# A fused gated recurrence and soft mixture of experts on one core: where two sigmoids stand in ScalarE's order, and a last weight loaded in three parts

## The chip, the cores and the metric

The kernel runs on one core of a Trainium2 chip. The metric is the time of one execution on the device, in microseconds (us). TensorE (PE, with its weight loads as PEld), VectorE (DVE), ScalarE (ACT) and GpSimd (POOL) each work through an order of their own; SyncE (SP) issues most of the transfers.

## The reference

For each of 4 batches of 5056 tokens with 256 channels, the first part is a recurrence along the tokens; the second part sends all 20224 tokens through 32 slots of 8 small experts and back.

```python
sig = 1.0 / (1.0 + np.exp(-f_logit))
f = lower_bound + (1.0 - lower_bound) * sig
i = 1.0 - f
for t in range(S):
    h = f[:, t] * h + i[:, t] * x[:, t]
    y[:, t] = h
...
logits = x @ phi                                # x: the recurrence's output, (20224, 256)
d = softmax of logits over the tokens           # each slot's weights
slot_input = d.T @ x
slot_out[e] = maximum(slot_input[e] @ w1[e], 0) @ w2[e]      # 8 experts, 4 slots each
c = softmax of logits over the 32 slots
out = c @ slot_out
```

## The kernel before

**Units.** The recurrence is cut into 40 units. A unit is a stretch of 512 tokens of one batch (`G`; `n_grp` is 10, and `B` is 4). Two units that are neighbours in number form a pair: one tile of logits `f_t`, one of `x_t` and one of gates `s_t` hold both of them. From unit 8 to 31 the units are "long" (`long`, line 177): a pair is 1024 neighbouring tokens of one batch, and each of its two tiles comes in one transfer (line 201). The tiles `f_t` and `x_t` have three buffers each.

**One unit's way through the engines.**

- `load` (line 194), for a pair, on SP's queue: `f_t`, then `x_t`. SP issues them in order; the one waits until a buffer of `f_t` is free, and that of `x_t` until one of `x_t` is.
- `gate` (line 217), on ACT, for a pair: the sigmoid of the negative logits into `s_t` (2048 elements in each partition).
- `enter` (line 227), on POOL, for each unit: `u_t = s_t * x_t`.
- `s_to_channels` (line 259) and `u_to_channels` (line 265), on PE: transposes of `s_t` and `u_t` into PSUM (`sp`, one buffer for a pair; `up`, two). For a long unit `u_to_channels` reads the `u_t` of both units of its pair (`half_to_channels`, line 253).
- `decay` (line 276), on ACT, for a pair: two instructions that make the decay `a` out of `sp` (line 285).
- `scan` (line 296), on DVE: two scans of 512 steps, out of `a` and `up`, into `h`.
- `to_tokens` (line 310), on PE, and `keep_tokens` (line 326), on DVE or ACT: `h` transposed back (`hp`, one buffer) and copied to `ht`. ACT has it for odd units, but for units with n mod 8 equal to 1 or 4 the two change places.
- `logits` (PE), `exps` (ACT, once for each two groups, line 356), `weights_to_tokens` (PE transposes `ep`, DVE copy `et`, line 371), `slots` (PE, line 397): the slot sums.

`idle` (line 170) and `spin` (line 142) issue matmuls whose results nobody reads.

**The order.** The instructions are issued in the order of the Python loop over n (line 469), and each engine keeps that order. In round n of the part that matters here, ACT gets: on an even n the gate of pair n+4, if n is at least `2 * B` = 8; on an odd n the decay of n+1 and then, if n is below 8, the gate of n+3. Then follow `exps` (for group 1 in round 9), and at the end of the round `keep_tokens(n - 1)`. POOL gets `enter(n + 3)`, then the weight loads that `W_AT` (line 148) names for this round. PE gets `to_tokens(n - 1)`; on an even n `s_to_channels` of n+2 and n+3; `u_to_channels(n + 1)`; `idle`; logits; and after the scan the transposes of the weights and the slot sums. Exps and sigmoids use different function tables of ACT, so a table load stands ahead of each change between them.

**The weights.** `load_w` (line 128) issues the 16 expert weights from POOL, one float32 array to one bf16 tile each. The last two go into a buffer of `f_t` (`w_t`). The last one, number 15, is loaded in two halves, of four chunks each along the hidden dimension (line 137). Six weights, 10 to 15, are issued in round 36; behind them POOL fills `hid` and `wide` with zeros (lines 565, 566) and copies `left` (line 390). Each half of weight 15 is read at the end of the expert part, by the matmuls of line 663: 16 for weight 14, then 16 for weight 15, two for each chunk, chunk 0 first.

**After that** all output rows are made in a stage of its own and stored (lines 687 to 793).

Of the kernel before, what the change touches and what calls it, by code (L numbers as in the profile page):

```python
# [18 lines left out]
def kernel(  # L19
# [11 lines left out]
    B, S, D = x.shape  # L31
    E = moe_w1.shape[0]
# [5 lines left out]
    FC = F // P  # L38
# [45 lines left out]
    def rep_constants(b):  # L84
        blk = ident_f[ds(b * NS, NS), ds(b * NS, NS)]
        nc.gpsimd.tensor_copy(rep[ds(b * NS, NS)], blk.unsqueeze(1).broadcast_to([NS, B, NS]))
# [41 lines left out]
    def load_w(i):  # L128
        if i < E:
            nc.gpsimd.dma_start(out=w1_sb[i], in_=w1_r[i])  # L130
        else:
            if i == 2 * E - 2:
                t = ld.tile([P, 2, R, D], F32, name="w_t", tag="f_t")
                t = t.rearrange("p u r d -> p (u r d)").bitcast(BF16).rearrange(
                    "p (e f d) -> p e f d", e=2, f=FC)
                w2_sb.extend(t[:, i] for i in range(2))
            k = FC // 2 if i == 2 * E - 1 else FC
            for f in range(0, FC, k):
                nc.gpsimd.dma_start(out=w2_sb[i - E][:, ds(f, k)], in_=w2_r[i - E][:, ds(f, k)])


# [13 lines left out]
    with tc.tile_pool(name="sp2", bufs=3) as sp2, \  # L155
# [38 lines left out]
        def load(n, k=2):  # L194
            for src, dst, tag in ((f_logit, fs, "f_t"), (x, xs, "x_t")):
                if n % 2 == 0:
                    dst[n // 2] = ld.tile([P, 2, R, D], F32, name=tag, tag=tag)
                t = dst[n // 2]
                if long(n):
                    g, b = place(n)  # L200
                    nc.sync.dma_start(
                        out=t.rearrange("p u r d -> p (u r) d"),
                        in_=src[b, ds(first(g), 2 * G)].rearrange("(p r) d -> p r d", r=2 * R))
                elif n // B == odd:
                    b, t0 = n % B, first(odd)
                    nc.sync.dma_start(
                        out=t[:, 0, R3],
                        in_=src[ds(b, 2), ds(t0 + P * R3, L)].rearrange("b t d -> t b d"))
                    for m in range(2):
                        nc.sync.dma_start(  # L210
                            out=t[:, m, ds(0, R3)],
                            in_=src[b + m, ds(t0, P * R3)].rearrange("(p r) d -> p r d", r=R3))
                else:
                    for m in range(n, n + k):
                        nc.sync.dma_start(out=t[:, ds(m % 2, 1)], in_=tokens(src, m, 1))

        def gate(n, k=2):
            if n % 2 == 0:
                sts[n // 2] = sp2.tile([P, 2, R, D], BF16, name="s_t", tag="s_t")
            s_t, f_t = sts[n // 2][:, ds(n % 2, k)], fs[n // 2][:, ds(n % 2, k)]  # L220
            if n // B == odd:
                m = (R + R3) * D
                s_t = s_t.rearrange("p u r d -> p (u r d)")[:, :m]
                f_t = f_t.rearrange("p u r d -> p (u r d)")[:, :m]
            nc.scalar.activation(s_t, f_t, ACT.Sigmoid, scale=-1.0)  # L225
# [33 lines left out]
        def s_to_channels(n):  # L259
            if n % 2 == 0:  # L260
                pss[n // 2] = psp.tile([P, 2, P, R], F32, name="sp", tag="sp")
            to_channels(n, pss[n // 2][:, n % 2], sts[n // 2][:, n % 2],
                        sts[n // 2][:, 0, R3])
# [88 lines left out]
        def exps(g):  # L352
            gs = batch_of(g)
            if g == gs[-1]:
                T = sum(rows(i) for i in gs) * R
                nc.scalar.activation(etall[:, ds(first(gs[0]), T)], lgs[0][:, :T], ACT.Exp,
                                     accum_out=csum[:, ds(g, 1)])
# [45 lines left out]
        def unit(f, m):  # L403
            if 0 <= m < n_unit:
                f(m)

        def group(f, m):
            if 0 <= m < n_unit and m % B == B - 1:
                f(m // B)
# [39 lines left out]
                                     skip_group_check=True)  # L449

        AHEAD = 6
        for n in range(SINGLE):
            load(n, 1)
        lb_constants()
# [14 lines left out]
        for n in range(n_unit):  # L469
            if n < SINGLE - 2:  # L470
                if n:
                    unit(to_tokens, n - 1)
                    unit(u_to_channels, n + 1)
                s_to_channels(n + 2)
                if n + 3 < SINGLE:
                    gate(n + 3, 1)
                decay(n + 2, 1)
                if n + 3 == SINGLE:
                    gate(n + 3)
                if n % 2 == 0:  # L480
                    unit(load, n + AHEAD)
                unit(enter, n + 3)
                rep_constants(n)
            else:
                end = n >= n_unit - 6
                if n % 2 == 0:
                    unit(load, n + AHEAD)
                    if n == SINGLE - 2:
                        to_tokens(n - 1)
                        keep_tokens(n - 1)  # L490
                    if not end and n >= 2 * B:
                        unit(gate, n + 4)
                else:
                    unit(decay, n + 1)
                    if n < 2 * B:
                        gate(n + 3)
                    if n == n_unit - 5:
                        gate(n + 3)
                        exps(odd - 1)
                if not end and n != n_unit - 7:  # L500
                    group(exps, n - 2)

                unit(enter, n + 3)
                for _ in range(W_AT.get(n, 0)):
                    load_w(w_next[0])
                    w_next[0] += 1

                if n == n_unit - 2:
                    unit(u_to_channels, n + 1)
                if n != SINGLE - 2:  # L510
                    unit(to_tokens, n - 1)
                if n == n_unit - 2:
                    keep_tokens(n - 1)
                if n % 2 == 0:
                    unit(s_to_channels, n + 2)
                    unit(s_to_channels, n + 3)
                if n != n_unit - 2:
                    unit(u_to_channels, n + 1)
                if n in (n_unit - 5, n_unit - 4):
                    idle(8)  # L520
                elif n == SINGLE - 2:
                    idle(4, True)
                elif n < n_unit - 4 and n % (2 * B) in (1, 5, 6, 7):
                    idle({6: 8, 7: 9}.get(n, 5 if n % 2 else 3))
                if n == n_unit - 2:
                    tail = psp.tile([P, 2, G], F32, name="tail", tag="sp")
                    rs_ps = tail[:, 0, ds(0, n_grp * R * B)].rearrange(
                        "p (q b) -> p q b", b=B)
                    late_ps, odd_ps = (
                        tail[:, 1].bitcast(BF16)[:, ds(i * R * P, R * P)].rearrange(  # L530
                            "p (r s) -> p r s", r=R) for i in range(2))
                    logits(odd)
                    exps(odd)
                    slots(odd - 1)
                    spin(tail[:, 1], 1, G)
                    odd_weights()
                elif not end and long(n - 1):
                    if n % B == 0:
                        g = (n - 1) // (2 * B) * 2
                        for i in range(2):  # L540
                            logits(g + i, [2, 3] if n % (2 * B) == 0 else [0, 1])
                elif not end:
                    group(logits, n - 1)
            if n == n_unit - 1:
                logits(last, [0, 1, 2])
                late_exps([0, 1, 2])
                row_sums(0)
                late_weights([0, 1, 2], nc.scalar.copy)

            unit(scan, n)  # L550
            if n not in (SINGLE - 2, n_unit - 2):
                unit(keep_tokens, n - 1)
            if n == n_unit - 3:
                weights_to_tokens(odd - 1)
                slots(odd - 2)
            elif not n >= n_unit - 6:
                group(weights_to_tokens, n - 3)
                batch(slots, n - 4, 0)
                batch(slots, n - 4, 1)
                if n > 2 * B and n % (2 * B) == 3:  # L560
                    idle(6)
# [126 lines left out]
    with tc.tile_pool(name="pout", bufs=4, space=PSUM) as pout, \  # L688
# [95 lines left out]
        end = len(blocks) - 1  # L784
# [39 lines left out]
```

## Time and profile before

| | |
|---|---|
| median of 4 runs | 200.77 us (200.63 to 202.54) |
| the profiled execution | 200.63 us, of which 198.9 us are the span from its first to its last instruction |
| mean granted TensorE clock | 0.855 |
| PE busy | 152.2 us (77%) |
| DVE busy | 143.3 us (72%) |
| ACT busy | 138.8 us (70%) |
| POOL busy | 102.6 us (52%) |
| DMA | 70.77 MB, 356 GB/s on the mean |
| the two scans' line 303, DVE, with and without a start value | 86.8 us and 9.4 us, some 1.2 us for each of 80 |

Read the times of a timeline as: start in us from the beginning of the span, how long, engine, line, operation, written tile and read tiles, shape, how many instructions lie in this row; in square brackets how long the engine was idle before, and what ended that. Rows of PE overlap a little, since matmuls are pipelined. In a row of windows each engine's busy time in that stretch stands with its number of instructions, then the granted TensorE clock, the DMA share and the GB/s.

### The profile page before, as it was taken

How to read it: one execution, taken by the hardware profiler on the slowest of the kernel's cores; microseconds unless marked ns; L12 is line 12 of the kernel's file. 1: busy time of each engine (PE TensorE's matmuls, PEld its weight loads, DVE VectorE, ACT ScalarE, POOL GpSimd, SP SyncE). 2: the span in 40 equal slices, each digit the busy share in tenths (PEclk: the TensorE clock that was granted, in tenths of full speed). 3: DMA queues.
4: the chain of work that ended last, by engine and by line, in shares of the span. 5: the costliest groups of instructions: out<-in, count | busy, mean ns of one | idle time of the engine just before them, and what ended most of it. 6: DMA issues, size and time to landing. Idle time of an engine off the chain costs nothing.

```text
span 198.9 us, 3495 instructions
## 1 busy us (share of the span) xinstructions
PE 152.2 (77%) x1330; PEld 108.8 (55%) x1330; DVE 143.3 (72%) x164; ACT 138.8 (70%) x195; POOL 102.6 (52%) x77
## 2 busy tenths in 40 slices
PE   0587496988998989899897987989989999960000
PEld 0365375766785767667685866667953633310000
DVE  1669888489989999999989999634158877850000
ACT  3688679499999998999997595623067889990000
POOL 2489577984987788874969969650030000000000
PEclk9999969699999999999999999999985555555555
DMA  6999999999999999999999999999429999999995
GB/s 181 413 419 422 428 428 424 424 427 343 397 432 419 415 328 420 430 408 323 398 419 391 226 213 213 214 215 210 84 95 419 424 440 422 422 448 438 428 422 214
DMA packets 14304, 70.77 MB, mean 356 GB/s; under 512 B 1728, under 2 KB 2752, under 8 KB 10320
## 3 DMA queue, kind: packets, MB, share of 16 engines
q1 hardware_dynamic: 11664, 62.13, 75.7%
q0 software_dynamic: 2480, 8.42, 21.2%
q8 instruction: 10, 0.16, 0.3%
q14 instruction: 6, 0.05, 0.1%
q10 hardware_dynamic: 144, 0.00, 0.0%
HBM read 58.23 MB, written 20.71 MB: 397 GB/s over the span
## 4 chain that ended last, share of the span: by engine, by line
PE 45%; DVE 25%; DMA 8%; issue 4%; ACT 4%; POOL 2%; SPq 0%; ACTq 0%; DVEq 0%; POOLq 0%
DVE h L303 18%; PE op L751 12%; DMA f_t<-in_f_logit_dram 8%; PE hp L316 5%; DVE ht L333 5%; PE sp L251 5%; PE up L257 4%; PE lg L347 3%; PE slot_ps L173 2%; PE op L702 2%; POOL u_t L236 2%; PE so_ps L663 2%; PE tail L144 2%; PE slot_ps L397 2%; ACT oc L762 1%
## 5 line engine op out<-in xcount | busy, mean ns | idle before, releaser
L236 POOL TENSOR_TENSOR u_t<-s_t,x_t 128x1024 bf16<-128x1024 bf16 (+1 forms) x39 | 82.5, 2127 | 24.3 <-ACT s_t L225 9.6
L303 DVE TENSOR_TENSOR_SCAN h<-a,h,up 128x512 bf16<-128x512 f32 (+1 forms) x72 | 86.8, 1251 | 6.0 <-PE up L257 4.8
L225 ACT ACTIVATE s_t<-f_t 128x2048 bf16<-128x2048 f32 (+2 forms) x23 | 38.4, 1669 | 7.9 <-DMA f_t<-in_f_logit_dram 7.4
L316 PE MATMUL hp<-ident_f,h 128*128 128x128 f32 (+1 forms) x160 | 29.8, 311 | 9.1 <-DVE ht L333 7.8
L316 PEld LDWEIGHTS hp<-ident_f,h 128*128 128x128 f32 (+1 forms) x160 | 23.0, 208 | 17.6 <-DVE ht L333 12.5
L251 PE MATMUL sp<-ident_f,s_t 128*128 128x128 f32 x144 | 21.2, 290 | 10.5 <-ACT s_t L225 7.9
L285 ACT ACTIVATE a<-sp,nomlb 128x1024 f32<-128x1024 bf16 x24 | 25.4, 1113 | 0.8 <-PE sp L251 0.6
L751 PE MATMUL op<-slot_bd,etall 64*128 64x512 bf16 x62 | 25.0, 621 | 0.3 <-ACT oc L762 0.2
L762 ACT ACTIVATE oc<-op,rrow 128x256 f32<-128x256 f32 x60 | 22.7, 486 | 2.1 <-PE op L751 1.6
L251 PEld LDWEIGHTS sp<-ident_f,s_t 128*128 128x128 f32 x144 | 17.4, 150 | 12.2 <-issue 5.9
L756 DVE TENSOR_TENSOR oc<-op,rrow 128x1024 f32<-128x1024 f32 x16 | 19.3, 1222 | 5.3 <-PE op L751 5.3
L292 ACT ACTIVATE a<-sp,nomlb 128x512 f32<-128x512 bf16 (+2 forms) x22 | 17.8, 857 | 3.9 <-PE sp L251 3.5
L257 PE MATMUL up<-ident_f,u_t 64*128 64x64 f32 x192 | 17.2, 229 | 2.2 <-POOL u_t L236 2.2
L751 PEld LDWEIGHTS <-etall 64*128 64x128 bf16 x62 | 9.0, 155 | 14.8 <-issue 12.7
L173 PE MATMUL slot_ps<-rep,ident 128*128 128x256 bf16 x115 | 17.1, 285 | 0.0
L257 PEld LDWEIGHTS up<-ident_f,u_t 64*128 64x128 f32 x192 | 13.7, 138 | 5.9 <-POOL u_t L236 2.5
L333 ACT COPY ht<-hp 128x512 f32<-128x512 f32 (+1 forms) x18 | 10.5, 581 | 7.5 <-PE hp L316 7.4
L333 DVE COPY ht<-hp 128x512 f32<-128x512 f32 (+1 forms) x22 | 14.7, 667 | 0.8 <-PE hp L316 0.8
L173 PEld LDWEIGHTS <-ident 128*128 128x128 bf16 x119 | 10.9, 103 | 2.8 <-issue 0.6
L303 DVE TENSOR_TENSOR_SCAN h<-a,up 128x512 bf16<-128x512 f32 x8 | 9.4, 1210 | 2.6 <-ACT a L292 1.9
L347 PE MATMUL lg<-h,phi 128*32 128x512 bf16 (+1 forms) x80 | 10.1, 412 | 0.0
L251 PE MATMUL up<-ident_f,u_t 128*128 128x128 f32 x48 | 9.3, 324 | 0.8 <-POOL u_t L236 0.8
(105 smaller groups left out, 147.9 us busy)
## 6 DMA issues: line engine op xcount, KB each, us to landing
f_t<-in_f_logit_dram SPq DMA_DIRECT2D x12, 1024.0 KB, 13.0
x_t<-in_x_dram SPq DMA_DIRECT2D x12, 1024.0 KB, 11.4
out_dram<-oc SPq DMA_DIRECT2D x6, 2048.0 KB, 12.8
w_sb<-in_moe_w_dram POOLq DMA_DIRECT2D x14, 512.0 KB, 9.7
f_t<-in_f_logit_dram SPq DMA_DIRECT2D x12, 512.0 KB, 8.7
x_t<-in_x_dram SPq DMA_DIRECT2D x12, 512.0 KB, 9.0
out_dram<-oc SPq DMA_DIRECT2D x4, 896.0 KB, 5.3
out_dram<-ob SPq DMA_DIRECT2D x1, 2048.0 KB, 8.5
```

The costliest lines, as they stand in the source:

```text
L173: nc.tensor.matmul(slot_bank[:, 1, ds(0, rhs.shape[1])], ident, rhs, start=first and i < 2, stop=False, skip_group_check=True)
L225: nc.scalar.activation(s_t, f_t, ACT.Sigmoid, scale=-1.0)
L236: nc.gpsimd.tensor_tensor(uts[n][:, :r], s_t[:, :r], x_t[:, :r], ALU.mult)
L251: nc.tensor.transpose(ps[:, :, r], t[:, r], ident_f)
L257: nc.tensor.transpose(v[:, :, r], t(r)[k].bitcast(F32), ident_f[k, k])
L285: nc.scalar.activation(a, sp[:, :, :, :, o], ACT.Identity, scale=nomlb[:, ds(o, 1)], bias=1.0)
L303: nc.vector.tensor_tensor_scan(h[:, :T, o], decays[n // 2, o][:, n % 2, :T], up[:, :T, o], hs[number(g - 1, b)][:, ds(used(g - 1) - 1, 1), ...
L316: nc.tensor.transpose(hp[:n_p, r], hw[:, :n_p, r], ident_f)
L333: copy(hts[g][:n_p, b].rearrange("p r d -> p (r d)").bitcast(F32), hps.pop(n)[:n_p].rearrange("p r c -> p (r c)"))
L751: nc.tensor.matmul(op[:, i_r].rearrange("p u d -> p (u d)"), ew[:, :, r + i_r], slot_bd[ds(j * 2 * NS, 2 * NS)].rearrange("s u d -> s (u d)"),
L756: nc.vector.tensor_tensor(ob[:, :, ds(r, k)].rearrange("p u r d -> p r u d"), op[:, ds(0, k)], scale[:, ds(r, k)].unsqueeze(3).broadcast_t ...
L762: nc.scalar.activation(ob[:, u, r + i_r], op[:, i_r, u], ACT.Copy, scale=scale[:, r + i_r, ds(u, 1)])
```

## The change

Two edits. The bound up to which the gates stand in odd rounds, behind the decay, goes from 8 to 12: so `gate(12)` moves from round 8 (ahead of all else on ACT in that round) to round 9, behind `decay(10)` and ahead of `exps(1)`; `gate(14)` moves from round 10 to round 11, behind `decay(12)`. From round 12 on the order is as before. And the last weight's two loads of four chunks each become three, of four, two and two chunks.

```diff
-            k = FC // 2 if i == 2 * E - 1 else FC
-            for f in range(0, FC, k):
+            parts = (FC // 2, FC // 4, FC // 4) if i == 2 * E - 1 else (FC,)
+            for j, k in enumerate(parts):
+                f = sum(parts[:j])
                 nc.gpsimd.dma_start(out=w2_sb[i - E][:, ds(f, k)], in_=w2_r[i - E][:, ds(f, k)])
...
         AHEAD = 6
+        SETTLED = 3 * B
...
-                    if not end and n >= 2 * B:
+                    if not end and n >= SETTLED:
                         unit(gate, n + 4)
                 else:
                     unit(decay, n + 1)
-                    if n < 2 * B:
+                    if n < SETTLED:
                         gate(n + 3)
```

## The prediction

> I read the chain of waits first, then the timelines of DVE, ACT, POOL and PE between 30 and 60 us, where the moved instructions stand, then the issues with their landings, and last the end of the expert part.
>
> **What bounds the kernel now.** From 40.28 us to the last scan at 126.7 us DVE has hardly a gap. Its timeline:
>
> ```profile
> 35.75 2.45 DVE L303 TENSOR_TENSOR_SCAN h<-a,h,up 128x512 bf16<-128x512 f32 x2 [1.49 <-PE up L257]
> 40.28 2.45 DVE L303 TENSOR_TENSOR_SCAN h<-a,h,up 128x512 bf16<-128x512 f32 x2 [2.08 <-PE up L257]
> 43.23 2.45 DVE L303 TENSOR_TENSOR_SCAN h<-a,h,up 128x512 bf16<-128x512 f32 x2
> 49.79 4.89 DVE L303 TENSOR_TENSOR_SCAN h<-a,h,up 128x512 bf16<-128x512 f32 x4
> 55.08 5.03 DVE L303 TENSOR_TENSOR_SCAN h<-a,h,up 128x512 bf16<-128x512 f32 x4 [0.39 <-PE up L257]
> ```
>
> These are scans 8, 9, 10, then 12 with 13, then 14 with 15. Later idle times are 0.40 us at 77.83 and 0.40 us at 100.58, no others of note. What DVE loses before that stretch or in it comes out at the end; what it could gain is the 2.08 and the 0.39. The 2.08 belongs to PE: behind the late u_t of unit 9 (35.13) it runs nine idle matmuls, hp, sp and up without a gap until 40.2, and nothing of that waits for ACT. The order on ACT:
>
> ```profile
> 33.02 1.91 ACT L225 ACTIVATE s_t<-f_t 128x2048 bf16<-128x2048 f32 x1 [0.18 <-POOL u_t L236]
> 37.90 1.91 ACT L225 ACTIVATE s_t<-f_t 128x2048 bf16<-128x2048 f32 x1 [2.97 <-DMA f_t<-in_f_logit_dram]
> 39.71 0.57 ACT L333 COPY ht<-hp 128x512 f32<-128x512 f32 x1
> 40.18 2.12 ACT L285 ACTIVATE a<-sp,nomlb 128x1024 f32<-128x1024 bf16 x2
> 42.32 1.28 ACT L356 ACT_TABLE_LOAD   x1
> ...
> 44.75 1.28 ACT L225 ACT_TABLE_LOAD   x1
> 46.04 1.91 ACT L225 ACTIVATE s_t<-f_t 128x2048 bf16<-128x2048 f32 x1
> 47.86 2.10 ACT L285 ACTIVATE a<-sp,nomlb 128x1024 f32<-128x1024 bf16 x2
> 49.85 1.91 ACT L225 ACTIVATE s_t<-f_t 128x2048 bf16<-128x2048 f32 x1
> ```
>
> That is gate 10; gate 12, which waits 2.97 us for its logits; keep 7; decay 10; exps 1 between two table loads; gate 14; decay 12; gate 16. Behind gate 12's wait stand keep 7 and decay 10. Does anybody wait for them? Scan 10 needs decay 10 and starts at 43.23, at once behind DVE's own work; decay 10 was begun at 40.18. So the wait costs nothing, and taking it out gains nothing on DVE's path.
>
> **The gates' new places, on ACT.** Gate 10 ends at 34.93. Keep 7 needs hp, which PE ends at 38.53: 38.57 to 39.14. Decay 10 needs sp (39.61): 39.65 to 41.77, 0.5 earlier than before. Gate 12 now follows: 41.67 to 43.58 (before: to 39.81), late by 3.8. Exps 1 with its load (2.40 from row to row) starts at 43.6 instead of 42.32 and ends at 46.0, late by 1.3. Decay 12 follows: 46.0 to 48.1, when it ended at 49.96 before. Then the second table load, 1.28, and gate 14: 49.41 to 51.32, against 47.95: late by 3.4. Gate 16 ends at 53.1, late by 1.35. The net of it is ACT time: the wait that gate 12 filled before, while PE made hp and sp, now stands empty until 38.57.
>
> The Trainium skill speaks here against the change: "ScalarE: Activation LUTs", section "What ACT_TABLE_LOAD costs", puts a switch at about 2.66 us, the load and a drain. By that price gate 14 would be late by some 1.4 more for each of the two switches that are now ahead of it on the late path. But the row shows 42.32 to the exponential at 43.61, 1.29 in all, so I take 1.28.
>
> **What waits for the gates.** POOL:
>
> ```profile
> 43.12 2.16 POOL L236 TENSOR_TENSOR u_t<-s_t,x_t 128x1024 bf16<-128x1024 bf16 x1
> 48.08 4.26 POOL L236 TENSOR_TENSOR u_t<-s_t,x_t 128x1024 bf16<-128x1024 bf16 x2 [2.81 <-ACT s_t L225]
> ```
>
> Enter 12 stood at 40.38; it goes to 43.65 to 45.78. Behind it are a weight load (0.61), then enter 13 (before 43.12 to 45.28): 46.4 to 48.55. PE's transposes of u_t 12 need both; they began at 46.99 and would end at 49.0. DVE wants them only when it is through with keep 10: hidden, by some 1 us. Exps 1, late by 1.3, holds PE's transposes of the weights (45.56) until 46.0 and DVE's copy et (46.24) until 46.6: DVE is late by 0.4 from here. Scan 12 at 50.2; scan 13 needs sp of 14 ahead of it on PE, and that needs gate 14 (51.32): up 13 ends at 52.9 and scan 13 starts at 53.0.
>
> Now units 14 and 15. POOL's row of 4.26 us starts 0.13 behind gate 14: 51.45 to 55.71, against 52.34. PE wanted them in this row:
>
> ```profile
> 54.27 0.70 PE L257 MATMUL up<-ident_f,u_t 64*128 64x64 f32 x8
> ```
>
> So 1.9 of the 3.4 us are covered and the rest is not. Four of the eight transposes need the second u_t: 55.75 and 0.4 more, and scan 14 starts at 56.25 instead of 55.08: **+1.2 us**. The 0.4 above lies within it, not on top. PE's up 15 follows by the same steps as before (idle, hp, sp, up), scan 15 starts at 58.8 instead of 57.65, also +1.2. Enter 17 is done at 60.0, ahead of where DVE needs up 16 (61.8): POOL has caught up. From then on DVE is full again, and its small waits at 77.83 and 100.58 end a loop that starts with DVE's own copies, so I count on no recovery.
>
> **The transfers that the gates release.** f_t 18 waits for gate 12: issued at 43.6, not 40.24. x_t 18 for enter 13: 48.6, not 45.30. f_t 20 for gate 14: 51.4, not 47.98. x_t 20 for enter 15: 55.7, not 52.37, and f_t 22 behind it in SP's order. All are 3.3 us late. They had landed 14.8, 12.2, 11.9 and 9.9 us after their issue, one every 2.4 us, with the DMA share at 1.0: they stood in line. x_t 20 would be served from 59.9; issued at 55.7 it still stands in line for 4 us. So I cost it at nothing; were there a hole, it moves all later landings, the weights' too, by its size.
>
> **The last weight.** The end of the expert part in the chain, and the landing of the second half, issued at 125.97:
>
> ```profile
> 142.96 1.79 PE so_ps L663 x32
> ```
>
> ```profile
> DMA to landing us min/median/max: 18.0/18.0/18.0
> ```
>
> So it lands at 144.0, and by the trace its first matmul starts at 144.13, without a gap. No wait to remove, then. The load is issued only when weight 8 has landed (1.64 us idle on POOL before it); the third load takes the next turn, and waits for weight 9, which lands at 128.1. POOL thus issues it at about 128.2, 2 us later, and ends the zeros of wide at some 133.4 (before 130.92), where they are read from 136.77: hidden, 3.4 us to spare. Two packet sizes bound the landing: packets of 4 KB of this queue took 0.324 us and of 2 KB 0.173 in the trace, so some 0.02 of each is fixed. One DMA engine works alone at the end; eight packets of 2 KB there become sixteen of 1 KB, +0.2 us. The last quarter is needed four matmuls, 0.22 us, later than the half was. The edit is worth nothing, between -0.1 and +0.1; and with PE late by 1.2 us it has that much slack.
>
> **Sum.** 1.2 + 0 + 0 = +1.2 us on the profiled execution: its span 198.9 goes to 200.1, its 200.63 to 201.8. The median is 0.14 above it: **202.0 us**.
>
> **Rivals.** *PE's clock falls.* The windows:
>
> ```profile
> 21.76:25.17 3.41, 1.48 (x14) 1.29 (x14) 3.05 (x3) 2.23 (x3) 1.24 (x2) 1.00 1.03 432
> 25.17:28.58 3.41, 3.41 (x23) 2.31 (x22) 2.96 (x3) 3.41 (x3) 3.27 (x3) 0.50 1.01 428
> 45.65:49.06 3.41, 3.25 (x42) 2.36 (x42) 3.41 (x5) 3.40 (x4) 0.98 (x1) 1.00 1.04 323
> ```
>
> PE was busy for 1.48 of 3.41 us, and the clock was 0.50 in the next window; with 2.41 busy (18.34 to 21.76) it stayed at 1.00. The skill's "TensorE: Matmul & The Clock Gate", section "HAM oscillation — how this bites in real kernels", says that gaps up to 3.4 us are harmless; the row shows a loss after a gap of 1.93, and the row decides. With the new waits (0.4 for the exps, 1.2 for enter 13) the window from 45.65 falls from 3.25 to about 2.0 busy, between the two known ones. If that halves the clock from 49.06 to 52.48, six idle matmuls cost 0.6 more (nine took 2.03 us at half clock at 35.6, five 0.65 at full), the slot sums at twice their 0.54 us 0.5, hp and sp 0.5 together (0.85 and 1.08 for 0.48 and 0.87); most of it ends while PE would wait for gate 14, and scan 14 slips another 0.5: +1.7, 202.5 us. By the page alone it stays 202.0.
>
> *A hole in the transfers.* If a lead of 4 us is not enough, landings slip; the last weight has 1.2 + 0.1 of slack, so a hole of 2.5 us costs 1.2 more: 203.2 us. Against it: at 95.55 a transfer of half the size landed in 6.6 us while landings followed without a hole.
>
> *Part of it is absorbed.* If the later 0.40 us waits do yield, two of them leave +0.4: 201.2 us.
>
> *Not slower.* Gate 12 must land its logits before keep 7 and decay 10 can go. If in the timed runs f_t 12 lands later than the 37.79 of this profile, the kernel before stalls DVE and the changed one doesn't. It starts to cost from 1.9 us of lateness (decay 10 may slip from 40.18 to 42.1), and outweighs the 1.2 from 3.1; at 4 it gives 199.9 us. Against it: the profiled execution is within 0.14 of the median, so no such lateness is in the time.
>
> **Chances.** My forecast (201.6 to 202.4) 0.45; clock or hole, 202.4 to 203.5, 0.25; absorbed, 200.5 to 201.6, 0.20; not slower by the logits' lateness, below 200.5, 0.10. The range leaves out the last case and the top of the second: 200.6 to 203.2. One per cent, 2.0 us, is about what a measurement of this kernel can tell from no change; the forecast itself is within it. Slower by more than that (above 202.8) takes the upper half of the second case and a little more for stalls that I don't see: 0.23. Faster by more needs most of the last case: 0.06. The same: 0.71.
>
> **What would show it.** Gate 12 near 41.7 and gate 14 near 49.4 us on ACT, with ACT idle from 34.9 to 38.6; enter 14 near 51.4 on POOL; DVE idle by about 0.7 us ahead of scan 14, at 56.25; the loads of x_t and f_t for units 18 to 22 issued 3.3 us later, but landings 2.4 us apart as before; POOL idle twice for weight landings, near 124 and 127; no gap ahead of line 663. It is wrong if scan 14 is not late (then POOL or ACT had more slack), if the shift is gone before 126.7 us (DVE is not the bound), or if landings spread (transfers are).

## The result, and the profile after

The changed kernel takes 200.85 us (median of 43 runs, 200.07 to 202.82), the kernel before, measured along with it, 201.52 us (64 runs). The ratio, which is one of means, is 0.9977, 95% interval 0.9962 to 0.9993: a little faster, where I forecast a little slower. All ratios here leave out runs over 1.5% above the lowest of their kernel: three of 22 with the bound at 16, two of six with the bound at 32, six of 22 of the second kernel without the last weights.

Executions of one kernel differ by up to 2.8 us, so one profile can mislead, as it did me. Their times fall into groups. Of the kernel before, 32 of 64 took 201.75 us or more, and none between 201.29 and 201.75; of the changed kernel, 7 of 43 took 202.28 or more, and none between 201.40 and 202.28. The means of the lower groups are 200.86 and 200.77, only 0.09 apart. So the gain of 0.46 us in the mean is that fewer executions take the longer times. The profiled execution of the changed kernel took 201.25 us (span 199.5), and belongs to its lower group.

Line numbers are one higher than before behind line 137, two higher behind line 451. ACT in the profile after:

```profile
33.04 1.91 ACT L226 ACTIVATE s_t<-f_t 128x2048 bf16<-128x2048 f32 x1
35.77 0.59 ACT L334 COPY ht<-hp 128x512 f32<-128x512 f32 x1 [0.82 <-PE hp L317]
36.69 2.12 ACT L286 ACTIVATE a<-sp,nomlb 128x1024 f32<-128x1024 bf16 x2 [0.34 <-PE sp L252]
38.70 1.91 ACT L226 ACTIVATE s_t<-f_t 128x2048 bf16<-128x2048 f32 x1
40.63 1.28 ACT L357 ACT_TABLE_LOAD   x1
...
46.36 3.71 ACT L226 ACTIVATE s_t<-f_t 128x2048 bf16<-128x2048 f32 x2
...
55.26 1.91 ACT L226 ACTIVATE s_t<-f_t 128x2048 bf16<-128x2048 f32 x1 [2.22 <-DMA f_t<-in_f_logit_dram]
```

Gate 10, keep 7 and decay 10, gate 12, the exps, gates 14 and 16, gate 18. Gate 12 no longer waits for its logits (they land at 37.6). But keep 7 runs at 35.8 and decay 10 at 36.7, 3 us ahead of my figures of 38.6 and 39.7: PE and DVE are earlier in this execution than in the profile before. DVE:

```profile
37.29 2.45 DVE L304 TENSOR_TENSOR_SCAN h<-a,h,up 128x512 bf16<-128x512 f32 x2 [0.33 <-PE up L258]
40.27 2.46 DVE L304 TENSOR_TENSOR_SCAN h<-a,h,up 128x512 bf16<-128x512 f32 x2
...
47.32 2.44 DVE L304 TENSOR_TENSOR_SCAN h<-a,h,up 128x512 bf16<-128x512 f32 x2
50.09 2.46 DVE L304 TENSOR_TENSOR_SCAN h<-a,h,up 128x512 bf16<-128x512 f32 x2 [0.33 <-PE up L258]
53.30 5.03 DVE L304 TENSOR_TENSOR_SCAN h<-a,h,up 128x512 bf16<-128x512 f32 x4 [0.75 <-PE up L258]
...
63.25 2.45 DVE L304 TENSOR_TENSOR_SCAN h<-a,h,up 128x512 bf16<-128x512 f32 x2 [1.17 <-PE up L258]
```

Scans 9 and 10 start 3.0 us earlier than in the profile before (40.28, 43.23), scan 12 by 2.5. The idle 0.75 ahead of scan 14 is the stall that I forecast; the lead shrinks to 1.8 (53.30 against 55.08). By scan 18 it is gone (66.20 against 65.99), because gate 18 now waits 2.22 us for its logits, with keep 13 behind it, on which hp of the next unit waits on PE:

```profile
57.70 0.77 PE L317 MATMUL hp<-ident_f,h 128*128 128x128 f32 x4 [1.43 <-ACT ht L334]
```

and PE's clock is half in the stretch that follows, in the view by windows:

```profile
54.90:58.30 3.40, 1.97 (x18) 1.40 (x16) 3.28 (x3) 3.04 (x3) 2.84 (x2) 1.00 1.02 431
58.30:61.70 3.40, 3.40 (x21) 2.94 (x20) 2.79 (x4) 3.26 (x4) 3.40 (x2) 0.50 1.02 426
```

Where did the 3 us come from, in work that the change doesn't touch? x_t of unit 8, issued at 16.5 in both, landed at 28.83 us here and at 30.68 in the profile before. POOL's enter 8 started at 29.4 instead of 30.8, PE's clock stayed full where it had been half from 35.4 to 38.8. That can't be the change: gate 12 comes later. So the question for the experiments was what the kernel before does when x_t 8 lands early.

### The profile page after: what moved, and what is told of

Its sections match the earlier page's. It is cut to its first block, busy times and chain, and to the rows that moved or that the text cites. A ratio compares the mean times of both kernels' runs of the same rounds, so it can differ in the third digit from the quotient of the medians.

```text
span 199.5 us, 3496 instructions
## 1 busy us (share of the span) xinstructions
PE 152.8 (77%) x1330; PEld 110.2 (55%) x1330; DVE 143.2 (72%) x164; ACT 138.5 (69%) x195; POOL 103.2 (52%) x78
## 4 chain that ended last, share of the span: by engine, by line
PE 38%; DMA 22%; DVE 19%; POOL 4%; issue 4%; ACT 1%; ACTq 0%; SPq 0%; DVEq 0%; POOLq 0%
DMA x_t<-in_x_dram 15%; DVE h L304 13%; PE op L753 12%; DMA f_t<-in_f_logit_dram 7%; POOL u_t L237 4%; PE hp L317 4%; DVE ht L334 3%; PE up L258 3%; PE sp L252 2%; PE op L704 2%; PE so_ps L665 2%; PE tail L145 2%; PE lg L348 2%; PE slot_ps L174 1%; PE slot_ps L398 1%
## 5 line engine op out<-in xcount | busy, mean ns | idle before, releaser
L252 PE MATMUL sp<-ident_f,s_t 128*128 128x128 f32 x144 | 22.1, 298 | 9.7 <-ACT s_t L226 7.7
L753 PE MATMUL op<-slot_bd,etall 64*128 64x512 bf16 x62 | 24.3, 592 | 0.3
L252 PEld LDWEIGHTS sp<-ident_f,s_t 128*128 128x128 f32 x144 | 18.0, 154 | 11.4 <-issue 5.9
L258 PE MATMUL up<-ident_f,u_t 64*128 64x64 f32 x192 | 18.2, 233 | 2.5 <-POOL u_t L237 2.5
L258 PEld LDWEIGHTS up<-ident_f,u_t 64*128 64x128 f32 x192 | 14.3, 141 | 6.5 <-POOL u_t L237 3.1
```

The source lines that it names most:

```text
L252: nc.tensor.transpose(ps[:, :, r], t[:, r], ident_f)
L258: nc.tensor.transpose(v[:, :, r], t(r)[k].bitcast(F32), ident_f[k, k])
L753: nc.tensor.matmul(op[:, i_r].rearrange("p u d -> p (u d)"), ew[:, :, r + i_r], slot_bd[ds(j * 2 * NS, 2 * NS)].rearrange("s u d -> s (u d)"),
```

## The experiments

Ratios are to the kernel before, timed along with each set, with 95% intervals. The two theories in the expectations: A, the moved gates make the gain; B, the third load does. "Last scan" is the start of the last unit's scan.

**The kernel before, once more.**

> The kernel before, once more, for its profile and as a measure of what no change gives: 1.000 within 0.002. Theory A: if x_t of unit 8 lands near 28.8 us here, scan 9 starts near 37.3 and scan 10 stalls behind decay 10 by about 1 us (decay 10 starts at 40.1 as before); if it lands at 30.7, no stall. Theory B says nothing about this stretch.

Ratio 1.0005 (0.9982 to 1.0028), as it should be. The profile gave what was missing: x_t 8 landed at 28.82. ACT and then PE:

```profile
37.74 1.91 ACT L225 ACTIVATE s_t<-f_t 128x2048 bf16<-128x2048 f32 x1 [2.98 <-DMA f_t<-in_f_logit_dram]
39.55 0.57 ACT L333 COPY ht<-hp 128x512 f32<-128x512 f32 x1
40.02 2.12 ACT L285 ACTIVATE a<-sp,nomlb 128x1024 f32<-128x1024 bf16 x2
```

```profile
36.96 0.64 PE L347 MATMUL lg<-h,phi 128*32 128x512 bf16 x8
40.17 0.75 PE L316 MATMUL hp<-ident_f,h 128*128 128x128 f32 x4 [2.58 <-ACT ht L333]
```

ACT is the same as in the first profile to within 0.2 us; it is pinned to the landing of f_t 12. But hp has one buffer, and hp 8 waits for keep 7, which stands behind gate 12: PE idles 2.58 us, DVE 1.44, and then the clock is half. In the first profile hp 8 came without a wait, behind PE's own late work, 0.46 us after keep 7 had ended (40.28):

```profile
40.74 0.75 PE L316 MATMUL hp<-ident_f,h 128*128 128x128 f32 x4
```

DVE and the windows of the repeat:

```profile
40.96 0.69 DVE L333 COPY ht<-hp 128x512 f32<-128x512 f32 x1 [1.44 <-PE hp L316]
41.69 2.45 DVE L303 TENSOR_TENSOR_SCAN h<-a,h,up 128x512 bf16<-128x512 f32 x2
...
46.38 0.69 DVE L371 COPY et<-ep 128x1024 bf16<-128x1024 bf16 x1 [1.66 <-PE ep L368]
...
49.93 4.89 DVE L303 TENSOR_TENSOR_SCAN h<-a,h,up 128x512 bf16<-128x512 f32 x4
```

```profile
38.00:41.40 3.40, 1.23 (x12) 1.11 (x12) 1.96 (x3) 3.40 (x4) 2.79 (x2) 1.00 1.02 431
41.40:44.80 3.40, 3.40 (x19) 3.06 (x18) 3.29 (x4) 3.35 (x5) 3.37 (x3) 0.50 1.01 429
```

1.23 of 3.40 us busy, then half clock. Scan 10 starts at 41.69, not at 40.27 as in the profile after, and scan 12 at 49.93, not 47.32. Scan 10 stood behind keep 8 and so behind hp 8, not behind decay 10 as I expected. The loads alone (below), with the old gates and the early landing, show the same: 42.48 and 50.91, with 6.8 us at half clock. Against expectation there is a second stall, 1.66 us ahead of et, larger than the first. With the clock held (below) it is 0.60; so some 1.1 us of it is the half-clock stretch.

The longer stretch of half clock seems to make a group of its own in the times. The profiled run of the loads alone took 201.85 us, its last scan starting at 125.51 instead of 124.48. Between 201.5 and 202.25 us lie 21 of the 64 runs of the kernel before, 3 of 22 of this repeat, 6 of 22 of the loads alone; with gate 12 moved none of 43 of the change, none of 14 of the gates alone, none of 22 of gate 12 alone. That the group is of this kind is inferred from the one profile that lies in it.

**The gates alone; the loads alone.** The first keeps the two halves of the last weight, the second keeps the bound at 8.

```diff
-            parts = (FC // 2, FC // 4, FC // 4) if i == 2 * E - 1 else (FC,)
-            for j, k in enumerate(parts):
-                f = sum(parts[:j])
+            k = FC // 2 if i == 2 * E - 1 else FC
+            for f in range(0, FC, k):
```

> The gates' edit alone (bound 12), the last weight still in two halves. Theory A (gates): in executions in which x_t of unit 8 lands early (28.8 us as in the profile after, not 30.7 as in that of before), gate 12's wait for its logits holds keep 7 and decay 10 and costs some 1 us, and the moved gate saves it: then this kernel has the whole gain, ratio to before 0.997 to 0.998. Theory B (weights): the gain comes from the last weight's smaller last part: then this kernel is at 1.000 or, as I predicted, above it, up to 1.006.

> The three loads alone, all gates as before. Theory A (gates): 1.000, and no gap ahead of line 663 in either. Theory B (weights): 0.997 to 0.998, since the last half lands at 144.0 us whatever the rest does, and a PE that is early waits for it; the last of three parts is needed four matmuls (0.22 us) later.

Gates alone: 0.9996 (0.9968 to 1.0024). Loads alone: 1.0004 (0.9978 to 1.0029). Neither theory by itself, as far as these intervals can tell. The trace of the first shows where a lead can end: its last scan starts at 123.16 us, 1.3 earlier than the 124.48 of the repeat, but PE then waits for the last half:

```profile
141.60 1.80 PE L664 MATMUL so_ps<-w_t,wide 128*128 128x128 bf16 x24
144.00 0.61 PE L664 MATMUL so_ps<-w_t,wide 128*128 128x128 bf16 x8 [0.60 <-DMA w_t<-in_moe_w_dram]
```

The last weight lands at 143.85 to 144.01 us in each of these kernels whatever DVE does. A lead on DVE's path ends at this line. In the profile before, 0.12 us of slack stood there: it sat just above this floor.

**Of the gates only gate 12** (bound 10, three loads).

> Of the gates' edit gate 12 alone is moved behind decay 10 (bound 10; gate 14 stands in round 10 as before); three loads. In two profiles of kernels with the old gates, scan 10 stalled behind decay 10 by 1.8 and 2.6 us and scan 11 by another 1.8 and 2.0. Theory A (gate 12's wait for its logits costs the kernel before, gate 14 only follows): scan 10 starts near 40.6 us as in the kernels with both moved, ratio to before 0.997 to 0.999, as the change. Rival (it is gate 14 that matters): scan 10 without a stall, but scan 11 late by 2 us as before, ratio 1.000.

0.9970 (0.9946 to 0.9993), like the change. Scan 10 at 40.56, scan 11 at 44.69, last scan at 123.08. So of the two gates it is gate 12 that matters; moving gate 14 too adds nothing that shows. And here is what the third load is for:

```profile
141.52 1.05 PE L665 MATMUL so_ps<-w_t,wide 128*128 128x128 bf16 x16
142.75 0.99 PE L665 MATMUL so_ps<-w_t,wide 128*128 128x128 bf16 x12 [0.18 <-DMA w_t<-in_moe_w_dram]
144.00 0.38 PE L665 MATMUL so_ps<-w_t,wide 128*128 128x128 bf16 x4 [0.26 <-DMA w_t<-in_moe_w_dram]
```

Four matmuls are left behind the last landing instead of eight; the last starts at 144.17, against 144.39 with two halves.

**The last two weights not loaded**, with the old and the new gates.

```diff
-            if i == 2 * E - 2:
+            if i >= 2 * E - 2:
+                w2_sb.append(w2_sb[E - 3])
+                return
...
```

> The kernel before with the last two weights not loaded: the matmuls of experts 6 and 7 read expert 5's second weight instead, so two of eight experts compute with a wrong weight; all instructions but the three loads stay. Theory C (the stream of transfers ends the expert part: the last weight lands at 143.9 to 144.0 us in all six profiles, whatever DVE did): with the stream ending 4.8 us earlier this kernel follows DVE alone: 0.998 to 1.001 of before, since DVE was at most some 0.3 us ahead of the weights there. Rival (weights never bind): 1.000.

> The same omission (the last two weights not loaded, experts 6 and 7 read another's weight) with the gates of the change. Theory C: DVE is 1.3 us ahead at the last scan with the moved gates (123.16 against 124.48 us in two profiles), and here nothing holds it at the end: ratio to before 0.993 to 0.995, and lower than the one without the moved gates by 0.004 to 0.007. Rival (the gates' lead is lost on the way, or isn't real): the two shortened kernels agree within 0.002.

0.9977 (0.9953 to 1.0001) and 0.9963 (0.9937 to 0.9988): the difference that I expected is not there. Over all 22 runs of each the two means are 201.21 and 201.25 us, the same. Four of the second kernel's runs took 199.28 to 199.81 us, the others 200.88 and more; its profile is of one of the others, with the half clock at 58 us and the last scan at 124.63. That the four are executions that keep the lead past gate 18 is a guess; no trace shows one. As a measure of the floor this was inconclusive.

**More late gates.** The bound at 16, at 32, and gates 12 and 18 alone.

```diff
-        SETTLED = 3 * B
+        SETTLED = 4 * B          # then 8 * B
```

> The bound at 16 instead of 12 (the gates of units 16 and 18 too behind their decays), three loads. Theory A: in the profile after, gate 18 waited 2.22 us for its logits with keep 13 behind it, PE stood for 1.43 us and its clock fell; with the gate behind decay 16 that stall is gone: ratio to before 0.994 to 0.997, below that of the change. My prediction's reasoning (a later gate is only late): 1.002 to 1.008. Transfers as the bound at this place: the same as the change, 0.9977.

> The bound at 32: all gates up to that of unit 34 stand behind their decay, three loads. Theory A with my prediction's working for a stretch in which DVE is full and no gate waits for its logits: each period of eight units then has its gate late by some 3 us, POOL's u_t late, scans late by about 1 us in each of the two later periods: last scan 2 us later than with the bound at 16, ratio 1.003 to 1.010. Rival (a later gate costs nothing anywhere, ACT only needs to be spared the wait): 0.997.

> Of all gates only 12 and 18 stand behind their decays, the two that wait for their logits in the profiles (2.98 and 2.2 us); 14 and 16 as before; three loads. If what counts is only to spare ACT's order the waits for logits, this is at or below the bound at 16: ratio to before 0.994 to 0.997, scan 18 near 64.7 us and no half clock near 58 us. If a late gate 18 costs as much as its wait, it is as gate 12 alone, 0.997.

Bound 16: 0.9969 (0.9947 to 0.9991), or 0.9983 by the means over all 22 runs; not separable from the change. Bound 32: 1.0186 (1.0140 to 1.0232), worse than I had put it. Its profile is of its longest run, 208.40 us against a median of 205.58; there scan 18 to 26 takes 24.4 us (22.75 in the profile before) and the last weight lands at 151.89, but where the other runs lose their time isn't shown. Gates 12 and 18: 0.9981 (0.9958 to 1.0004); gate 18 moved behind decay 16 ran at 58.1 instead of 55.2, no half clock near 58, last scan at 123.54: no better than gate 12 alone.

**x_t of unit 8 made late**, with the old and the new gates.

```diff
-                    unit(load, n + AHEAD)
+                    load(n + AHEAD, of=[0] if n == 2 else range(2))
...
-                    unit(load, n + AHEAD)
+                    if n == SINGLE - 2:
+                        load(n + AHEAD, of=[0])
+                        load(n + AHEAD - 2, of=[1])
+                        load(n + AHEAD, of=[1])
...
```

Round 2 loads f_t 8 alone; round 4 (`SINGLE` is 6) loads f_t 10, x_t 8 and x_t 10, in this order.

> The kernel before, but x_t of unit 8 is issued behind f_t of unit 10 on SP, so that it lands some 2 to 4 us later (31 to 33 us, against 28.8). This makes always what the profile before happened to show (30.7). Scan 8 near 36 to 38 us. By my prediction's working gate 12's wait is then hidden behind PE's late work: PE doesn't wait for keep 7, no half clock at 39 to 46 us. Ratio to before 1.000 to 1.006.

> The same late x_t of unit 8, with the change's gates and three loads. Theory A, with my prediction's working for this condition: gate 12 near 41.7 or later, gate 14 near 49.4, scan 14 later than in the kernel with the old gates and the same late x_t by about 1 us; ratio to before above that one by 0.003 to 0.007. Rival (the moved gates help in every condition): below that one by 0.002 or more.

1.0092 (1.0061 to 1.0122) and 1.0162 (1.0127 to 1.0198): with a late x_t 8 the change makes the kernel slower, by 1.3 us between the medians (203.44 and 204.75). DVE with the old gates, then with the new:

```profile
43.24 2.45 DVE L304 TENSOR_TENSOR_SCAN h<-a,h,up 128x512 bf16<-128x512 f32 x2 [2.70 <-PE up L258]
...
52.74 4.89 DVE L304 TENSOR_TENSOR_SCAN h<-a,h,up 128x512 bf16<-128x512 f32 x4
58.03 5.03 DVE L304 TENSOR_TENSOR_SCAN h<-a,h,up 128x512 bf16<-128x512 f32 x4 [0.40 <-PE up L258]
```

```profile
43.48 2.45 DVE L305 TENSOR_TENSOR_SCAN h<-a,h,up 128x512 bf16<-128x512 f32 x2 [3.05 <-PE up L259]
...
55.96 2.46 DVE L305 TENSOR_TENSOR_SCAN h<-a,h,up 128x512 bf16<-128x512 f32 x2 [0.33 <-PE up L259]
59.16 5.03 DVE L305 TENSOR_TENSOR_SCAN h<-a,h,up 128x512 bf16<-128x512 f32 x4 [0.75 <-PE up L259]
```

Scan 14 is late by 1.13 us, the last scan by 1.10 (128.46, 127.36). This is about my +1.2, in a condition near the one that I had taken for the usual: x_t 8 lands at 32.85 and 32.73 us here, 2 us later than in the profile before. PE's clock was half from 35.6 to 42.4 in the one and from 36.4 to 43.2 in the other; I had expected less cost for the late landing alone, up to 1.006.

**The wait kept, the clock held.** Old gates, two halves, and 16 idle matmuls where PE stood still.

```diff
+                if n == 2 * B + 1:
+                    idle(16)
                 if n != SINGLE - 2:
                     unit(to_tokens, n - 1)
```

> The kernel before with 16 more idle matmuls (some 2.1 us) on PE ahead of hp 8 in round 9, where PE stood still for 2.6 and 2.8 us in the profiles with the old gates, waiting for keep 7 behind gate 12; its clock fell in the window after. Theory D (the price of gate 12's wait is PE's clock falling, more than the late copies themselves): no half clock between 38 and 46 us, ratio to before 0.996 to 0.999, near the change. Theory E (the price is the wait itself: scan 10 behind decay 10): 1.000, since decay 10 still starts at 40.0.

> The old gates with 16 idle matmuls in round 9 once more, for a profile in which x_t of unit 8 lands early (28.8 us; its first profile had 30.5, where PE did not wait). Theory D: hp 8 near 40.1 us still behind keep 7, but no half clock between 38 and 46 us, idle matmuls in 0.11 us each, scan 10 near 41.5 and scan 12 near 48.5 to 49.5, last scan near 123.1 to 124.0 (124.5 with the old gates alone); ratio 0.993 to 0.997. Theory E: last scan at 124.5, ratio 1.000.

0.9946 (0.9917 to 0.9975), and the second time 0.9934 (0.9914 to 0.9953): more than the change gains, but not for the reason tested alone. In the first profile x_t 8 landed at 30.52 and PE did not wait there; the matmuls were in its way, and the last scan started at 125.06, against 124.36 in the profile before. The second profile has the early landing. PE, DVE and the windows in it:

```profile
38.19 1.92 PE L173 MATMUL slot_ps<-rep,ident 128*128 128x256 bf16 x16
40.28 0.75 PE L316 MATMUL hp<-ident_f,h 128*128 128x128 f32 x4 [0.17 <-ACT ht L333]
```

```profile
45.41 0.69 DVE L371 COPY et<-ep 128x1024 bf16<-128x1024 bf16 x1 [0.60 <-PE ep L368]
...
48.95 2.45 DVE L303 TENSOR_TENSOR_SCAN h<-a,h,up 128x512 bf16<-128x512 f32 x2
```

```profile
37.40:40.90 3.50, 3.33 (x33) 2.32 (x31) 2.48 (x3) 3.06 (x3) 2.94 (x3) 1.00 0.99 419
40.90:44.30 3.40, 3.40 (x35) 2.93 (x33) 3.22 (x4) 3.37 (x4) 3.37 (x3) 1.00 1.02 431
```

hp 8 is as late as ever (40.28), gate 12 waits as ever, scan 10 starts at 41.77 as ever. But scan 12 starts at 48.95 instead of 49.93, and the last scan at 123.86 instead of 124.48. With gate 12 moved alone they start at 47.63 and 123.08. So at scan 12 the half clock is 1.0 us of a price of 2.3, at the last scan 0.6 of 1.4; the wait itself is the larger part.

The rest of the gain in time arises elsewhere. From the start of the last expert matmul to the end the profiles with added idle matmuls (four in all, two of them below) took 53.80 to 53.82 us, the other 13 profiles 54.32 to 54.88. SP's issue of the second output transfer, in the repeat of the kernel before and in the second profile here:

```profile
148.26 1.55 SPq L728 DMA_DIRECT2D out_dram<-ob  x1
```

```profile
146.49 0.42 SPq L730 DMA_DIRECT2D out_dram<-ob  x1
```

It takes 0.42 or 0.43 us in these four, 1.07 to 1.56 in the 13. So, by the profiles, 0.5 to 1.1 of the 1.3 us that these matmuls gain in the mean the second time (201.52 to 200.21) lies 100 us behind the wait that they fill. It came in the first profile too, where PE did not wait. Why the issue is shorter was not tested; matmuls added at a place without a wait would have told the two apart.

**Both findings together**: the idle matmuls with the three loads and old gates; and the change with 10 idle matmuls ahead of hp 14 (round 15), its own remaining wait.

> The old gates with 16 idle matmuls ahead of hp 8 in round 9, and the last weight in three loads: the two things that the runs so far point to. Theory D: as the kernel with the idle matmuls alone (0.9946) or up to 0.001 below it, since the last part is needed four matmuls later; below the change (0.9977). If that 0.9946 was luck of 12 runs, it is 0.997 to 0.999.

> The change with 10 idle matmuls (1.3 us) on PE ahead of hp 14 in round 15, where in its profile PE stood for 1.43 us behind gate 18 and the clock was half from 58.3 to 61.7. Theory D: that half clock is gone, last scan near 123.1 instead of 124.6, ratio to before 0.994 to 0.997. If the wait itself is what costs there, it is as the change, 0.9977.

0.9917 (0.9891 to 0.9943), 199.79 us, the lowest of all; and 0.9948 (0.9925 to 0.9972), 200.22 us. Both have the shorter output stage, so these ratios too are not what the wait and the clock are worth. In the second's PE timeline the wait is filled:

```profile
56.82 1.59 PE L174 MATMUL slot_ps<-rep,ident 128*128 128x256 bf16 x13
58.25 0.65 PE L317 MATMUL hp<-ident_f,h 128*128 128x128 f32 x4
```

No half clock near 58, and the last scan at 123.64 instead of 124.56: this part is the clock's and the wait's.

## Why the prediction was wrong, point by point

- **The step that failed**: "So the wait costs nothing, and taking it out gains nothing on DVE's path." I had asked who waits for keep 7 and decay 10, and looked at scan 10 alone. In the profile that I had, x_t 8 was late, PE with it, and keep 7 was ready 0.46 us before PE came for hp 8. In the other, usual order of events (x_t 8 landed before 29 us in 12 of the 15 profiles that issue it at the old place) hp 8 on PE waits 2.58 us for keep 7, and the clock goes to half. My sum should have held, with a minus sign, what of this reaches the end: 1.4 us at the last scan (124.48 in the repeat, 123.08 with gate 12 moved), of which the last weight's landing leaves less. The last expert matmul starts 0.35 us earlier (144.17, against 144.52 in the profile before), and 1.5 us earlier than where two windows of half clock follow the wait (145.67, the loads alone).
- **"From 40.28 us ... DVE has hardly a gap"** was true of that execution and read as a law. With the early landing the kernel before has gaps of 1.44 and 1.66 us there.
- **The +1.2 us** holds under a condition like the one assumed: 1.1 us at the last scan, 1.3 in time, when x_t 8 is made late. The profile after shows its trace too (idle 0.33 and 0.75 ahead of scans 13 and 14), paid out of a lead of 3.
- **The transfers**: right that the landings don't move, f_t 18 at 54.85 against 55.01; but those for units 18 to 22 were issued later by up to 0.4 us only, not 3.3 (the whole stretch ran early). What I left out is the other side: that landing binds. Who runs ahead of the transfers waits for f_t 18, and with the half clock behind it this took back the whole lead in the profile after. With the gates alone, whose gates stand in the same places, PE's clock stayed full there, scan 18 started at 64.78 instead of 66.20, and 1.3 us were left at the last scan.
- **The last weight**: right that there was no wait to remove, in that execution, and right about POOL (idle 1.27 and 1.89 us for landings, hidden). But I called it worth nothing, between -0.1 and +0.1. With PE ahead it is worth 0.22 us at the last matmul (144.17 against 144.39), four matmuls that no longer follow the last landing; in the profile after PE was not ahead, and it was worth nothing.
- **The rivals**: "not slower" had the right place, gate 12's wait with keep 7 and decay 10 behind it, but the wrong trigger. f_t 12 landed at 37.6 to 37.8 in all profiles; it is not the logits that came later but the rest that came earlier. "PE's clock falls" I had held against the changed kernel; the kernel before suffers from it at gate 12's wait, and the changed one, in the profile after, at gate 18's.
- **The level**: the median of 4 runs, 200.77, was low for the kernel before: over 64 it is 201.52. The measured 200.85 lies in my range by luck.

Open stays why x_t 8 lands at 28.8 or at 30.4 to 30.7 us. Also the repeat of the kernel before had a half clock from 130.2 to 133.6, behind a window of 3.20 us busy, which moved the matmuls of line 663 that read the last weights from 142.8 to 144.5; no other profile has one at this point, and none shows what makes the changed kernel's seven longest runs. And the gain as such is small beside its interval. That gate 12's wait makes the kernel before lose time is shown by the traces, and agrees with the runs between 201.5 and 202.25 us, which are missing wherever gate 12 is moved; that the third load adds to it is shown by single traces alone, since the ratios overlap.

## What to carry to other kernels

Before you cost a wait at nothing, name everybody behind it through single buffers (here keep 7, then hp, then PE, then DVE), and ask how early each could be, not only how early it was in the one profile. Look at how the times are spread before you explain a median: here the gain is a group of longer runs that is gone. A wait of an engine that feeds PE can cost more than itself if PE's clock falls in the window after, and idle matmuls in it can save that part. When an edit gains, find the stretch in which it does: much of what the idle matmuls gained lay in a stage that they were not meant for. And a lead gained early must still pass the transfers: look for the landing that doesn't move, and shorten what follows it.

## What the runs showed of the hardware

- PE's clock went to half for the next 3.4 us after windows of 3.4 us with 1.23, 1.48 and 1.97 us busy, the longest gap within them 2.19, 1.93 and 1.43 us; it stayed full after 2.29 (the gates alone, from 54.50 us). Gaps well below 3.4 us are thus not harmless, against the rule weighed in the prediction. No threshold comes out of the traces: the clock fell after 2.18 us busy (the change with idle matmuls, from 43.34) and even after 3.20 (the repeat, from 126.74), and stayed full after 1.82 (the loads alone, from 22.16) and 1.57 (x_t 8 late with the old gates, from 21.95).
- The last weight's last part landed at 143.8 to 144.1 us in the kernels that load all weights and keep the transfers in line, though the last scan's start moved by 2.4 us (123.08 to 125.51).
- With the last part 1 KB in each partition in place of 2 KB the last landing did not move visibly: 143.85 to 144.05 in seven profiles, 143.84 to 144.01 in five.
- SP's issue of the second output transfer took 0.42 or 0.43 us in the four profiles with added idle matmuls, 1.07 to 1.56 in the 13 others.
